# Local attention's product with v in four strips of 32 queries

## The chip, the cores and the metric

The kernel runs on one core of one Trainium2 chip. The metric is the device time of one execution in microseconds (us); lower is better. The core's engines are PE (TensorE, the matrix engine; PEld is its weight load, the load of the operand that stays in the array), DVE (VectorE), ACT (ScalarE), POOL (GpSimd) and SP (SyncE, which issues the transfers here).

## The reference

Three stages stand in a row: an attention with a sliding window, a mixture of eight dense experts, and one more two-layer network. Only the first is touched. For 4 batches and 8 heads there are 512 local and 32 global positions with a head width of 64. A local query sees the 32 global keys and the local keys at most 32 positions away:

```python
mask = np.abs(pos[:, None] - pos[None, :]) <= window
s_ll = np.where(mask, s_ll, -1000000000.0)
s_l = np.concatenate([s_lg, s_ll], axis=-1)
a_l = sm(s_l)
out_l = np.matmul(a_l, np.concatenate([v_g, v_l], axis=2))
```

The 32 global queries of each head see all 544 keys.

## The kernel before

**The attention.** The 32 (batch, head) pairs are called heads here, numbered t = 0 to 31. The 512 local queries of a head are four tiles of 128 (i = 0 to 3). For a tile, `scores` (L233, L234) makes the products with a stretch of 192 or 224 keys into the tile `s`; `maxi` (L245, DVE) adds the mask and takes the maximum; `expo` (L253, ACT) writes the exponentials `e`; `transp` (L299) transposes `e` on PE in two blocks of 112 keys into `ptp`, and a copy (L304 on ACT, L306 on DVE) brings them to `pt`. `pv` (L309) then multiplies: for each of the two blocks j, `pt` with its 112 keys by 128 queries is the weight, and the block's rows of v with a column of ones (`vw`, 112 x 65) move through the array. The two products add up in `o`, which has 128 partitions (queries) by 4 tiles by 65. `onorm` copies `o` out (L335, DVE) and divides by the column of sums.

**The global queries.** `scores_g` (L274) multiplies a head's 32 global queries with 224 and then 320 keys into `sg`; its weight has 32 columns. It is written as a generator, and `pv` lets it go one matmul further after each of its own products. `global_pv` (L363), once for every four heads, multiplies with v in 20 matmuls of 32 weight columns, each into its own 32 partitions of `og`.

**The order.** Everything in the attention stands in an order written out by hand; each engine goes through its own instructions in that order. In turn t the loop over i takes `scores`, `maxi` and `expo` of head t, `transp` of head t - 1, `pv` of tiles 0 and 1 of head t - 1 (with `scores_g` of head t between the products), and `pv` of tiles 2 and 3 of head t - 2 (with nothing between). Between such steps `fill_for` puts matmuls of the first two expert units (L131, L133, L135, and the logits at L402), which have 256 or 512 moving columns; in the first turns there are matmuls on zeros instead (L522). The attention ends at about 252 us; the experts and the last network follow and use the same engine.

**Records.** The fp32 products of `pv` and `global_pv` stand in the trace as two weight loads and two matmuls each: L316 has 512 records for 256 matmuls, L363 has 320 for 160. The names with `kh`, `sq`, `x11h` and the like are fp32r and have one record each.

Of the kernel before, what the change touches and what calls it, by code (L numbers as in the profile page):

```python
# [60 lines left out]
def tile_net(ctx: ExitStack, tc, kq, vw, vc, qg, wg, w1, w2, wi, wo, consts, out):  # L61
    nc = tc.nc
# [246 lines left out]
    def pv(t, i, between=iter(())):  # L309
        s = st[t]  # L310
        if i == 0:
            s["o"] = pso.tile([128, 4, VN], F32, tag="o", name="o")
            s["v"] = vw_t.pop(t)
        pt = s["pt", i // 2]
        for j in range(2):
            nc.tensor.matmul(  # L316
                s["o"][:, i, :], pt[:, (i % 2) * 2 + j, :], s["v"][:, i, j, :], start=(j == 0), stop=(j == 1)
            )
            next(between, None)

    def norm(o, dst):
# [185 lines left out]
    with tc.manual_schedule():  # L507
# [49 lines left out]
        for t in range(nq + 2):  # L557
# [12 lines left out]
            for i in range(4):  # L570
# [20 lines left out]
                if i >= 2:  # L591
                    between = scores_g(t, i - 2) if 0 < t < nq else iter(())
                    if 0 <= t - 1 < nq:
                        pv(t - 1, i - 2, between)
                    for _ in between:
                        pass
                if i < 2 and 0 <= t - 2 < nq:
                    pv(t - 2, i + 2)
                    if i == 1:
                        onorm(t - 2)  # L600
# [568 lines left out]
    with tc.manual_schedule():  # L1169
# [30 lines left out]
        for a, ((p, u), after) in enumerate(zip(order, order[1:])):  # L1200
# [22 lines left out]
            elif a in BACK:  # L1223
                j = BACK.index(a)
# [72 lines left out]
        for k in range(len(turns) + 1):  # L1297
# [9 lines left out]
            if k in (2, 3):  # L1307
                s = xs_[k + 1]
                side2.extend([None] * 5 + s[:5] + [None, s[5], None, s[6]])
            per = -(-len(side2) // len(seq))  # L1310
            for e in seq:
                w, i = e[0], int(e[1])
# [94 lines left out]
```

## Time and profile before

| | |
|---|---|
| time, median of 3 runs | 1983.7 us (1981.88 to 1984.66) |
| time of the profiled execution | 1985.1 us |
| span of the profiled execution | 1983.3 us |
| PE busy | 1958.3 us (99%), 11099 records |
| PE weight load busy | 1708.5 us (86%) |
| DVE, ACT, POOL busy | 1521.0, 815.1, 762.4 us |

Matmuls overlap in the array, and a record reaches from a matmul's start to the end of its results. So a record's length says less than the distance from one record's start to the next one's start, and these distances are what is read below.

### The profile page before, as it was taken

The page shows a single profiled execution, that of the slowest core. Times are in us where ns is not written, and L with a number is a line of the kernel's source. Part 1 is how long each engine was busy: PE and PEld are TensorE (multiplying, and loading weights), DVE is VectorE, ACT ScalarE, POOL GpSimd, SP SyncE. Part 2 cuts the span into 40 slices and gives each one's busy share as a digit, 9 for nine tenths or more (in the row PEclk, how much of TensorE's full clock was granted, in tenths as well). Part 3 has the DMA queues.
Part 4 walks back from the last instruction along what each step waited for, and adds up shares of the span by engine and source line. Part 5 has one row for each costly group of instructions (what it writes and reads, how often), then busy time and mean ns, then how long its engine had stood idle before and what let it go on. Part 6 is the DMA issues. An engine that isn't in the chain of part 4 may idle for free. (4 is left out here: it accounts for less than half of the span.)

```text
span 1983.3 us, 30571 instructions
## 1 busy us (share of the span) xinstructions
PE 1958.3 (99%) x11099; PEld 1708.5 (86%) x11099; DVE 1521.0 (77%) x2864; ACT 815.1 (41%) x1683; POOL 762.4 (38%) x665
## 2 busy tenths in 40 slices
PE   8999899999999999999999999999999999999999
PEld 7898887888888888899999999999999977789998
DVE  7778767776777767778888787888888668878887
ACT  6655523332333323333333334333333335545664
POOL 6665512333232333325343544445455202223322
PEclk9999999999999999999999999999999999999999
DMA  7446451123322232453333333342333396554332
GB/s 234 139 134 216 122 202 64 64 74 97 117 88 97 70 102 82 155 181 102 114 100 123 91 123 104 115 137 79 120 90 114 112 299 177 168 196 157 118 118 69
DMA packets 204518, 251.01 MB, mean 127 GB/s; under 512 B 17232, under 2 KB 150096, under 8 KB 204368
## 3 DMA queue, kind: packets, MB, share of 16 engines
q1 hardware_dynamic: 204368, 249.06, 40.0%
q8 instruction: 87, 1.43, 0.3%
q14 instruction: 63, 0.52, 0.1%
HBM read 190.16 MB, written 58.85 MB: 126 GB/s over the span
## 5 line engine op out<-in xcount | busy, mean ns | idle before, releaser
L135 PE MATMUL m<-w2h,hl 128*128 128x512 f32 x1360 | 535.2, 394 | 2.5 <-POOL hl L1056 2.5
L131 PE MATMUL m<-w2h,hh 128*128 128x512 f32 x1360 | 534.0, 393 | 2.1 <-ACT hh L1055 2.1
L133 PE MATMUL m<-w2l,hh 128*128 128x512 f32 x1360 | 533.5, 392 | 0.0
L1025 ACT ACTIVATE hh<-t 128x288 fp32r<-128x288 f32 (+1 forms) x368 | 184.8, 502 | 432.1 <-DVE t L1019 429.5
L135 PEld LDWEIGHTS m<-w2h,hl 128*128 128x128 f32 x1360 | 255.7, 188 | 58.5 <-POOL hl L1056 6.0
L131 PEld LDWEIGHTS m<-w2h,hh 128*128 128x128 f32 x1360 | 255.9, 188 | 50.6 <-ACT hh L1055 2.6
L133 PEld LDWEIGHTS m<-w2l,hh 128*128 128x128 f32 x1360 | 255.9, 188 | 49.4
L1027 DVE SCALAR_TENSOR_TENSOR hl<-t,hh 128x288 fp32r<-128x288 f32 (+1 forms) x368 | 281.0, 764 | 5.2 <-ACT hh L1025 1.5
L127 POOL TENSOR_TENSOR w2l<-w2r,w2h 128x512 fp32r<-128x512 f32 x120 | 164.2, 1393 | 300.5 <-ACT w2h L123 285.7
L1127 DVE SCALAR_TENSOR_TENSOR acc<-m,pr,acc 128x512 f32<-128x512 f32 x247 | 183.2, 746 | 113.7 <-PE m L135 112.3
L1019 DVE TENSOR_TENSOR t<-q,u 128x288 f32<-128x288 f32 (+1 forms) x348 | 182.9, 526 | 62.3 <-PE q L1086 52.6
L1056 POOL TENSOR_TENSOR hl<-eg,hh 128x288 fp32r<-128x288 f32 (+2 forms) x112 | 102.7, 924 | 290.0 <-ACT hh L1055 193.0
L743 ACT CAST wh<-wt 128x512 fp32r<-128x512 f32 x120 | 68.9, 619 | 235.1 <-POOL wt L739 235.1
L739 POOL TENSOR_TENSOR wt<-w1r,wt 128x512 f32<-128x512 f32 x60 | 89.1, 1485 | 194.4 <-DVE hl L1027 101.8
L739 POOL TENSOR_TENSOR wt<-w1r 128x512 f32<-128x512 f32 x60 | 79.8, 1334 | 164.4 <-DVE hl L1027 122.1
L1067 DVE TENSOR_TENSOR u<-q,s 128x288 f32<-128x288 f32 (+1 forms) x116 | 61.2, 527 | 83.3 <-PE q L1086 60.0
L747 DVE TENSOR_TENSOR wl<-wt,wh 128x512 fp32r<-128x512 f32 x120 | 107.1, 903 | 12.8 <-ACT wh L743 11.0
L813 POOL TENSOR_TENSOR cp<-r,cp 128x512 f32<-128x512 f32 x32 | 42.6, 1332 | 144.4 <-DVE cp L803 78.2
L1275 DVE TENSOR_TENSOR acc<-m,acc 128x512 f32<-128x512 f32 x105 | 72.1, 688 | 33.0 <-PE m L135 32.9
L253 ACT ACTIVATE e<-s,m 128x192 f32<-128x192 f32 (+1 forms) x128 | 55.7, 437 | 75.5 <-DVE m L245 74.9
L316 PEld LDWEIGHTS o<-vw,pt 112*128 112x128 f32 x512 | 77.1, 194 | 10.4 <-issue 3.8
L316 PE MATMUL o<-vw,pt 112*128 112x65 f32 x512 | 78.7, 260 | 6.2 <-issue 3.6
(248 smaller groups left out, 4665.8 us busy)
## 6 DMA issues: line engine op xcount, KB each, us to landing
w1r<-in_w_dram SPq DMA_DIRECT2D x60, 512.0 KB, 5.3
w2r<-in_w_dram SPq DMA_DIRECT2D x60, 512.0 KB, 4.2
kq<-in_kq_dram SPq DMA_DIRECT2D x31, 544.0 KB, 4.0
wh<-wqh SPq DMA_DIRECT2D x98, 128.0 KB, 2.6
wl<-wql SPq DMA_DIRECT2D x98, 128.0 KB, 2.6
r<-in_wo_dram SPq DMA_DIRECT2D x16, 512.0 KB, 4.0
r<-in_wi_dram SPq DMA_DIRECT2D x16, 512.0 KB, 4.0
vw<-in_vw_dram SPq DMA_DIRECT2D x32, 227.5 KB, 4.8
```

The source lines that it names most:

```text
L127: e.tensor_tensor(out=lo, in0=src, in1=hi.bitcast(F32), op=ALU.subtract)
L131: nc.tensor.matmul(ps, ah, bh, start=first, stop=False)
L133: nc.tensor.matmul(ps, ah, bl, start=False, stop=False)
L135: nc.tensor.matmul(ps, al, bh, start=False, stop=last)
L316: nc.tensor.matmul(s["o"][:, i, :], pt[:, (i % 2) * 2 + j, :], s["v"][:, i, j, :], start=(j == 0), stop=(j == 1))
L739: eng.tensor_tensor(out=t, in0=get(a), in1=get(b), op=op)
L747: eng.tensor_tensor(out=wop[n + "l"], in0=src, in1=wop[n + "h"].bitcast(F32), op=ALU.subtract)
L1019: nc.vector.tensor_tensor(out=t, in0=ps, in1=rest, op=ALU.add)
L1025: nc.scalar.activation(hh, t, AF.Relu)
L1027: late.append(lambda: nc.vector.scalar_tensor_tensor(out=hl, in0=t, scalar=0.0, in1=hh.bitcast(F32), op0=ALU.max, op1=ALU.subtract))
L1056: nc.gpsimd.tensor_tensor(out=hl, in0=g[:, a:b], in1=hh.bitcast(F32), op=ALU.subtract)
L1127: nc.vector.scalar_tensor_tensor(out=accs[i], in0=ps, scalar=scale, in1=accs[i], op0=ALU.mult, op1=ALU.add)
```

## The change

Each matmul of `pv` becomes four. Matmul c takes the weight columns of 32 queries and writes the 32 partitions of `o` that belong to them; the moving operand is the same 112 x 65 block of v each time.

```diff
         for j in range(2):
-            nc.tensor.matmul(
-                s["o"][:, i, :], pt[:, (i % 2) * 2 + j, :], s["v"][:, i, j, :], start=(j == 0), stop=(j == 1)
-            )
+            for c in range(0, 128, 32):
+                nc.tensor.matmul(
+                    s["o"][c:c + 32, i, :], pt[:, (i % 2) * 2 + j, c:c + 32], s["v"][:, i, j, :],
+                    start=(j == 0), stop=(j == 1),
+                )
             next(between, None)
```

There are two forms of the place on PE. In the first, with `scores_g` between the products (62 of the 128 calls of `pv`), this is what stands on PE in turn 1; the line below `pv` moves from 316 to 317, and those behind it by two:

```order
 L299 MATMUL ptp<-ident,e_139 112x128 x2
-L316 MATMUL o<-vw,pt 128x65
+L317 MATMUL o<-vw,pt 32x65 x4
 L274 MATMUL sg<-kh,sqg 32x224
-L316 MATMUL o<-vw,pt 128x65
+L317 MATMUL o<-vw,pt 32x65 x4
 L274 MATMUL sg<-kl,sqg 32x224
```

Nothing moved: four matmuls of 32 partitions stand where one of 128 stood, and the matmuls of `scores_g` stand between the two fours. In the second form, with nothing between (the other 66 calls), PE has in turn 2:

```order
 L299 MATMUL ptp<-ident,e_140 112x128 x2
-L316 MATMUL o<-vw,pt 128x65 x2
-L522 MATMUL idle<-hl 128x512
+L317 MATMUL o<-vw,pt 32x65 x8
+L524 MATMUL idle<-hl 128x512
 L299 MATMUL ptp<-ident,e_140 112x128 x2
```

Eight stand in a row where two stood. On the other engines and in the transfers the order is the one before.

## Rows read from the trace of the kernel before

**Rows 1.** Busy time in stretches: start:end, length, busy us (records), granted clock, DMA.

```profile
20.00:252.00 232.00, 221.15 (x1989) 201.21 (x1989) 176.45 (x605) 137.28 (x315) 140.16 (x158) 0.99 0.51 158
...
1000.00:1983.00 983.00, 974.80 (x5483) 866.03 (x5481) 789.50 (x1367) 421.28 (x901) 364.62 (x307) 1.00 0.43 131
```

**Rows 2.** Groups with their shapes: records, busy us, mean ns, idle before.

```profile
L316 PE MATMUL o<-vw,pt 112*128 112x65 f32 x512 | 78.7, 260 | 6.2 <-issue 3.6 <-ACT pt L304 1.9 <-ACT e L253 0.6
...
L363 PE MATMUL og<-vc,ptg 112*32 112x65 f32 x256 | 5.3, 223 | 0.0
```

**Rows 3.** PE in order of time (start us, length us, records), `global_pv` behind 512 columns.

```profile
177.26 0.40 PE L131 MATMUL m<-w2h,hh 128*128 128x512 f32 x1
177.59 0.78 PE L363 MATMUL og<-vc,ptg 112*32 112x65 f32 x40
178.30 0.50 PE L133 MATMUL m<-w2l,hh 128*128 128x512 f32 x1
178.64 0.25 PE L233 MATMUL s<-kh,sq 128*128 128x192 f32 x1
```

**Rows 4.** The same view, `global_pv` behind 256 columns.

```profile
146.64 0.28 PE L133 MATMUL m<-x22l,wh 128*128 128x256 f32 x1
146.85 0.78 PE L363 MATMUL og<-vc,ptg 112*32 112x65 f32 x40
147.56 0.39 PE L135 MATMUL m<-x22h,wl 128*128 128x256 f32 x1
147.78 0.28 PE L131 MATMUL m<-x22h,wh 128*128 128x256 f32 x1
```

**Rows 5.** The same view, `global_pv` behind `scores_g`; then one weight load there.

```profile
57.60 0.34 PE L274 MATMUL sg<-kh,sqg 128*32 128x320 f32 x1
57.78 0.33 PE L316 MATMUL o<-vw,pt 112*128 112x65 f32 x2
57.92 0.34 PE L274 MATMUL sg<-kl,sqg 128*32 128x320 f32 x1
58.19 0.79 PE L363 MATMUL og<-vc,ptg 112*32 112x65 f32 x40
...
57.63 0.34 PEld L316 LDWEIGHTS o<-vw,pt 112*128 112x128 f32 x2
```

**Rows 6.** The same view, `pv` without `scores_g`, between 512 columns.

```profile
120.27 0.48 PE L133 MATMUL m<-w2l,hh 128*128 128x512 f32 x1
120.58 0.56 PE L316 MATMUL o<-vw,pt 112*128 112x65 f32 x4
120.94 0.47 PE L135 MATMUL m<-w2h,hl 128*128 128x512 f32 x1
121.26 0.27 PE L233 MATMUL s<-kh,sq 128*128 128x224 f32 x1
```

**Rows 7.** The same view, `pv` without `scores_g`, between 256 columns.

```profile
80.66 0.28 PE L131 MATMUL m<-x11h,wh 128*128 128x256 f32 x1
80.78 0.56 PE L316 MATMUL o<-vw,pt 112*128 112x65 f32 x4
81.14 0.36 PE L133 MATMUL m<-x11l,wh 128*128 128x256 f32 x1
81.34 0.27 PE L135 MATMUL m<-x11h,wl 128*128 128x256 f32 x1
```

**Rows 8.** The same view, two expert matmuls behind each other.

```profile
116.48 0.39 PE L131 MATMUL m<-w2h,hh 128*128 128x512 f32 x1
116.71 0.40 PE L133 MATMUL m<-w2l,hh 128*128 128x512 f32 x1
```

**Rows 9.** Waits of PE's weight load, 20 to 252 us: total, times, longest.

```profile
PEld o L316 <- issue: 3.8, 1, 3.8
...
PEld og L363 <- issue: 2.0, 7, 0.4
```

**Rows 10.** The view of rows 1, one stretch (granted clock behind the counts).

```profile
204.00:211.00 7.00, 6.36 (x32) 6.39 (x32) 5.03 (x19) 3.49 (x8) 3.50 (x4) 0.52 0.50 152
```

## The prediction

> **What bounds the kernel now.** I read the busy times by stretch first. From 20 to 252 us, where the attention runs, PE is busy 221.15 of 232 us, DVE 176.45, POOL 140.16, ACT 137.28 [rows 1]: PE has 10.9 us in which nothing runs on it, every other engine 55 us or more. Behind the attention PE is busy 974.80 of 983 us [rows 1]. So PE sets the pace in the stage of the change, and what it is late at 252 us it is late at the end; the order that follows is fixed and nothing in it waits for a clock time. Then I read PE in order of time around the products in question, start to start, since the records overlap: a record of `pv` is 260 ns long on average [rows 2], but four of them and the next matmul's start take 0.36 us [rows 6, 7].
>
> The kernel already holds the form that the change introduces. `global_pv` has the same moving operand (112 x 65), the same 32 weight columns and the same four strips, 40 records at a time [rows 2, 3]. Its rows price the change.
>
> **Prices from `global_pv`.** (a) Pace. From the first start to the last end it takes 0.78 us; a record is 0.22 us long, so the last starts 0.56 us behind the first: 39 steps of 14.4 ns [rows 2, 3]. (b) Way out. The next wide matmul starts at 0.71 us, 0.15 us behind the last start, and its successor 0.34 us later [rows 3] where 0.23 us is the usual distance of 512 columns [rows 8]: 0.11 us for a weight load that was not made ahead. With 256 columns it is 0.71 again, and 0.22 us [rows 4] against 0.12 [rows 7]. (c) Way in. The first strip starts 0.33 us behind a matmul of 512 columns, 0.21 behind one of 256, 0.27 behind a `scores_g` of 320 [rows 3 to 5]; usual are 0.23, 0.12 and 0.18 [rows 8, 7, 5]. The weight load waits there for nothing that the trace names: 2.0 us in 7 places, about 0.29 us each [rows 9]. I read this as the array running empty at each change between strips and full width.
>
> **The change, call by call.** `pv` is called 128 times. It removes 256 matmuls of full width (512 records) and adds 1,024 strips (2,048 records). No wait, no transfer and no work of another engine is added.
>
> 66 calls have nothing between their products. Before: after 512 columns 0.31 us to the first record, 0.36 us to the next wide matmul, 0.32 us to its successor [rows 6]; after 256 columns 0.12, 0.36, 0.20 [rows 7]. After: 16 records take 15 x 14.4 ns = 0.22 us and 0.15 us out, 0.37 together. So the run itself gains nothing, and the ends cost: 0.33 + 0.37 + 0.34 against 0.99 is +0.05 us; 0.21 + 0.37 + 0.22 against 0.68 is +0.12 us.
>
> 62 calls have a matmul of `scores_g` behind each product. The question is whether that matmul, with 32 weight columns too, counts as a strip. The trace says no: the full-width weight of `pv` is loaded at 57.63, 0.03 us behind the start of a `scores_g` at 57.60, so these two do not stand off from each other, while `global_pv` behind a `scores_g` starts 0.27 instead of 0.18 us later [rows 5]. Then each such call goes in and out twice. A run of two records and the step to `scores_g` took 0.14 us [rows 5]; 8 strips take 7 x 14.4 ns = 0.10 and 0.15 us out: +0.11 us, twice: 0.22. The second way in costs 0.27 - 0.18 = 0.09 us. The first costs 0.33 - 0.31 = 0.02 behind 512 columns and 0.21 - 0.12 = 0.09 behind 256. The load for `scores_g` after each way out is no longer hidden; no row shows it. It has a quarter of the columns of (b), so at least 0.03 us, and at most the full 0.11; I take 0.05, nearer to the quarter, twice: 0.10. Sum: +0.43 us behind 512 columns, +0.50 behind 256.
>
> What stands ahead of a call is 512 columns, 256 columns or a transpose of 128, for which no row shows a way in; I take the middle of the two known, 0.465 and 0.085 us. 62 x 0.465 + 66 x 0.085 = 28.8 + 5.6 = **34.4 us** more on PE. All calls as behind 512 columns: 62 x 0.43 + 66 x 0.05 = 30.0; all as behind 256: 62 x 0.50 + 66 x 0.12 = 38.9. The uncertain load moves this by 124 x 0.02 = 2.5 us down or 124 x 0.06 = 7.4 us up.
>
> Something of it falls into time in which PE waits today: 10.9 us at most [rows 1], of which 3.8 us is one wait for a late `vw` transfer [rows 9] that PE would reach later, and part of the rest is waits for copies and exponentials [rows 2] whose inputs PE makes itself and would make later too. I take 5 us, with 0 and 10.9 as ends. DVE (the copy of `o` out) gets its data a fraction of a us later and has 55 us to spare.
>
> So 34.4 - 5 = +29.4 us on the profiled execution, 1985.1 to 2014.5 us. The median of the runs is 1.4 us below the profiled one: **2013 us**. Ends: 30.0 - 2.5 - 10.9 = +16.6 gives 2000; 38.9 + 7.4 = +46.3 gives 2030.
>
> **Rivals.**
> 1. `scores_g` does count as a strip once the array is in strips. Then a call with it goes in once and out once: in 0.055 on average; two runs of 8 and a step, 0.115 instead of 0.14 us, -0.05; out behind the last `scores_g` 0.09 + 0.11 = 0.20. +0.205 x 62 + 5.6 = 18.3, less 3 hidden: 1999 us. For it: the same 32 columns. Against it: rows 5. Chance 0.12.
> 2. Faster: strips run side by side and the ends cost nothing. Then 16 starts at 14.4 ns are 0.23 us for 0.36, and two runs of 8 save 0.05: 66 x 0.13 + 62 x 0.05 = 11.7 us, 1972 us. There are 66 x 2 + 62 x 4 = 380 changes of width, so it turns into a loss once one costs over 11.7 / 380 = 0.03 us. For it is the pace of 14.4 ns; against it the ends of every row of `global_pv` [rows 3 to 5]. Chance 0.04. The Trainium skill (TensorE: Matmul & The Clock Gate, section "Part 3: Packing small matmuls") reports 2.38 times the speed for three column strips of 512 moving columns; the pace in rows 3 agrees that strips overlap, and here 65 columns leave the ends to decide.
> 3. PE is less of a bound than it looks. Overlapping records hide short waits, so more than the idle 10.9 us could give way; twice that, 21.8 us, leaves +12.6, 1996 us. Against it: no other engine is over 76% busy [rows 1]. Chance 0.10.
> 4. The clock. From 204 to 211 us the granted clock is 0.52 (the level of 1.2 GHz in nearly all of it) [rows 10], right behind the 3.8 us wait [rows 9]. More places where the array runs empty may bring more such stretches; each costs at most half of its 7 us. Three more give 2023 us; the loss of this one gives 3.5 us back. Chance 0.08.
> 5. Short runs do not reach the pace of the long one. Each ns more per start costs 2,048 ns; at twice the distance, 28.8 ns, that is 29.5 us, 2042 us. Against it: 40 starts in 0.56 us, which hold ten rounds of four strips [rows 3]. Chance 0.05. The Trainium skill (the same page, section "Wait — 56ns, not 53.3ns?") says that matmuls never start less than about 25 ns apart; by that the strips would take 2,048 x 10.6 ns = 21.7 us more, 2035 us. Rows 3 differ from it, and the measurement decides here.
>
> That nothing changes at all has 0.01: the order on PE shows the four strips at every call.
>
> **How the numbers follow.** The forecast has the remaining 0.60; its own range is that of its ends, 2000 to 2030 us. The range for 8 in 10 goes from 1996 (rival 3, with rival 1 inside) to 2030 (the upper end of the sum); outside are rivals 2 and 5 and the tails. This kernel's runs scatter by about 0.1%, so 0.2% (4 us) is about what can be told from no change: slower by more than that is the forecast with rivals 1, 3, 4 and 5, nearly all of it, 0.94; within it 0.02; faster 0.04.
>
> **What would show it.** Right: the strips' records start about 14 ns apart in runs of 16 and 8; the weight load behind each run starts some 0.15 us behind the last strip and is not made ahead, also that of `scores_g` between two runs; the step from `scores_g` to a strip is about 0.3 us for 320 columns; the attention ends near 281 instead of 252 us, and from there to the end the time is what it was. Wrong: a load of `scores_g` made while strips still run (rival 1), an end of the attention at or ahead of 252 us (rival 2), the delay made good by PE waits that vanish (rival 3), new stretches at the lower clock (rival 4), or starts well over 14 ns apart (rival 5).

## The result

The changed kernel takes 2002.26 us (median of 4 runs, 2001.45 to 2002.87), the kernel before in the same comparison 1982.84 us. The ratio is 1.0097, 95% interval 1.0079 to 1.0114: 19.4 us slower. The profiled execution takes 2001.45 us.

The page's line of the changed kernel with the busy times (us, share of the span, records) shows the 1,536 added records on PE (and on its weight load, which is 22 us less busy), while the other engines are as they were but for 2 us more on DVE:

```profile
PE 1979.6 (99%) x12635; PEld 1686.1 (84%) x12635; DVE 1523.4 (76%) x2864; ACT 815.0 (41%) x1683; POOL 762.4 (38%) x665
```

What a call costs is read from PE in order of time (start us, length us, records). After the change, a call with `scores_g` between its products:

```profile
81.11 0.28 PE L133 MATMUL m<-x11l,wh 128*128 128x256 f32 x1
81.32 0.32 PE L317 MATMUL o<-vw,pt 112*32 112x65 f32 x8
81.57 0.33 PE L274 MATMUL sg<-kh,sqg 128*32 128x320 f32 x1
81.83 0.32 PE L317 MATMUL o<-vw,pt 112*32 112x65 f32 x8
82.08 0.34 PE L274 MATMUL sg<-kl,sqg 128*32 128x320 f32 x1
82.26 0.28 PE L135 MATMUL m<-x11h,wl 128*128 128x256 f32 x1
```

The same call before, first and last row:

```profile
78.39 0.28 PE L133 MATMUL m<-x11l,wh 128*128 128x256 f32 x1
...
79.15 0.28 PE L135 MATMUL m<-x11h,wl 128*128 128x256 f32 x1
```

From the expert matmul ahead to the one behind it is 1.15 us after and 0.76 us before: +0.39 us. Two ways into the strips can be seen (81.11 to 81.32, and 81.57 to 81.83, where 0.12 and 0.18 us were usual) and two ways out (0.25 us from the start of a run to the next matmul, of which the eight starts take 0.10).

The weight loads (PEld) of the same stretch show where `scores_g` stands:

```profile
81.32 0.16 PEld L317 LDWEIGHTS o<-vw,pt 112*32 112x32 f32 x8
81.57 0.11 PEld L274 LDWEIGHTS sg<-kh,sqg 128*32 128x32 f32 x1
81.83 0.16 PEld L317 LDWEIGHTS o<-vw,pt 112*32 112x32 f32 x8 [0.16 <-issue]
82.08 0.11 PEld L274 LDWEIGHTS sg<-kl,sqg 128*32 128x32 f32 x1
82.11 0.19 PEld L135 LDWEIGHTS m<-x11h,wl 128*128 128x128 f32 x1
```

The load of `scores_g` starts with its matmul at 81.57 and 82.08, not ahead of it, and so do the strips' loads; but the full-width load at 82.11 follows 0.03 us behind the `scores_g` at 82.08. So `scores_g` counts as a full-width matmul here, on both sides of the strips. Over the whole attention the strips' loads wait for nothing that the trace names (total us, times, longest; one of these waits, 3.6 us, is for a late `vw` transfer):

```profile
PEld o L317 <- issue: 23.6, 99, 3.6
```

A call with nothing between, behind 256 columns and behind 512, after the change:

```profile
83.75 0.28 PE L131 MATMUL m<-x11h,wh 128*128 128x256 f32 x1
83.96 0.44 PE L317 MATMUL o<-vw,pt 112*32 112x65 f32 x16
84.33 0.38 PE L133 MATMUL m<-x11l,wh 128*128 128x256 f32 x1
84.55 0.28 PE L135 MATMUL m<-x11h,wl 128*128 128x256 f32 x1
...
128.35 0.48 PE L133 MATMUL m<-w2l,hh 128*128 128x512 f32 x1
128.76 0.44 PE L317 MATMUL o<-vw,pt 112*32 112x65 f32 x16
129.13 0.50 PE L135 MATMUL m<-w2h,hl 128*128 128x512 f32 x1
129.47 0.27 PE L233 MATMUL s<-kh,sq 128*128 128x224 f32 x1
```

From the first to the last row of each it is 0.80 us where [rows 7] have 0.68, and 1.12 us where [rows 6] have 0.99. The run itself (its start to the next full-width start) is 0.37 us, as forecast, where it was 0.36.

In all these rows the next start comes 0.07 us ahead of the recorded end of what stands before it, wherever strips follow full width or full width follows strips: 0.28 us long and 0.21 to the next start, 0.48 and 0.41, 0.33 and 0.26, 0.32 and 0.25, 0.44 and 0.37. Where nothing changes it comes 0.16 to 0.20 us ahead (0.28 and 0.12, 0.56 and 0.36 in [rows 7]). This fits an array that has to run nearly empty at a change; the recorded ends are modelled, so it stays a reading.

Over all calls, from the last matmul ahead to the second behind, paired with the same call of before, the medians are +0.39 us for the 62 and +0.115 us for the 66: 62 x 0.39 + 66 x 0.115 = 31.8 us of price on PE.

The last product of `pv` stands at 251.7 us before and at 269.1 us after, 17.4 us later. From there to the first matmul into `q` (L1084, now L1086) it is 32.0 us in both, and from that to PE's last matmul 1695.3 and 1694.4 us: the whole loss is made in the attention, and 0.9 us of it comes back later. So in the profiled pair some 14 of the 31.8 us were absorbed. The stretches between two runs of `global_pv` show where. Before (start:end, length, busy us of PE, PEld, DVE, ACT, POOL, then the granted clock):

```profile
33.31:58.19 24.88, 22.77 (x211) 19.63 (x210) 21.07 (x74) 17.54 (x40) 19.77 (x20) 1.00 0.58 181
58.19:87.31 29.12, 27.78 (x264) 25.53 (x263) 21.35 (x80) 18.95 (x44) 18.26 (x19) 1.00 0.48 151
87.31:177.59 90.28, 89.56 (x815) 83.00 (x815) 68.69 (x245) 52.72 (x124) 55.95 (x66) 1.00 0.49 146
177.59:249.04 71.45, 65.18 (x544) 58.67 (x543) 52.78 (x167) 38.30 (x87) 35.30 (x44) 0.95 0.53 166
```

After:

```profile
34.64:59.63 24.99, 24.70 (x402) 17.31 (x401) 19.94 (x72) 17.37 (x40) 18.70 (x19) 1.00 0.59 174
59.63:91.42 31.79, 31.21 (x457) 23.36 (x456) 21.07 (x78) 19.15 (x44) 17.89 (x19) 1.00 0.42 131
91.42:192.58 101.16, 100.75 (x1392) 76.50 (x1391) 72.00 (x245) 52.74 (x123) 56.00 (x66) 1.00 0.45 132
192.58:266.29 73.71, 69.73 (x928) 52.47 (x927) 52.36 (x167) 38.21 (x87) 35.54 (x44) 0.98 0.52 159
```

Four heads (8 calls of each kind) carry a price of 8 x 0.39 + 8 x 0.115 = 4.0 us; the four stretches hold 4, 4, 12 and 8 heads. The third, where PE was idle 0.7 of 90 us, grows by 10.9 of 12 us: almost the whole price. The second grows by 2.7 of 4.0 us. The first grows by 0.1 of 4.0 us, and its idle time falls from 2.1 to 0.3 us. The last grows by 2.3 of 8 us: its idle time falls from 6.3 to 4.0 us, and the clock gives back about 2 us: (1 - 0.95) x 71.45 = 3.6 us of clock were missing before [rows 10], (1 - 0.98) x 73.71 = 1.5 us after. Ahead of 33 us the delay is 1.3 us for a price of 3.8; there the kernel before had another stretch at the lower of the two clock levels, from 9.5 to 16.5 us at 0.51, which began in a wait of 2.2 us for `sqg`; the changed kernel, which waited 1.6 us there, had 1.00.

PE's waits in the attention show which of them went (total us, times, longest; `issue` where the trace names no instruction). Before:

```profile
PE o L316 <- issue: 3.6, 1, 3.6
PE ptp L299 <- DVE pt L306: 2.4, 6, 0.7
PE o L316 <- ACT pt L304: 1.9, 4, 0.8
```

After:

```profile
PE o L317 <- issue: 3.8, 2, 3.4
PE o L317 <- ACT pt L304: 0.8, 2, 0.5
PE ptp L299 <- DVE pt L306: 0.3, 2, 0.2
```

The wait for the late `vw` transfer stayed (the longest `issue`, 3.6 and 3.4 us): this transfer was issued 16.3 us later too. What shrank are the waits for the copies `pt` and the exponentials, from 6.0 to 1.1 us with the rows not shown. Such a wait costs more than its idle time: at 55.98 us before, a `scores_g` started 0.85 us behind the product ahead of it, of which 0.52 us show as idle, and after the change 0.25 us. Added up start to start, the 128 calls are 25.0 us longer and not 31.8, the steps into the transposes (L299) are 5.4 us shorter and all other steps 2.2 us shorter: 17.4 us.

The other three executions of the changed kernel had a mean clock of 0.997 to 0.998 instead of 0.999, and their times lie within 1.4 us of the profiled one. By the medians 12 of the 31.8 us were absorbed, and the clock can have given some 2 us of this (an estimate: 0.001 of 2000 us, since the executions of the kernel before have 0.996 to 0.998).

### The profile page after: what moved, and what is told of

Read it like the earlier page. It is cut to its first block, busy times and chain, and to the rows that moved or that the text cites. A ratio compares the mean times of both kernels' runs of the same rounds, so it can differ in the third digit from the quotient of the medians.

```text
span 1999.7 us, 33643 instructions
## 1 busy us (share of the span) xinstructions
PE 1979.6 (99%) x12635; PEld 1686.1 (84%) x12635; DVE 1523.4 (76%) x2864; ACT 815.0 (41%) x1683; POOL 762.4 (38%) x665
## 5 line engine op out<-in xcount | busy, mean ns | idle before, releaser
L1067 ACT COPY s<-q 128x288 f32<-128x288 f32 (+1 forms) x116 | 51.9, 447 | 74.9 <-PE q L1088 74.9
L1039 ACT ACTIVATE er<-t 128x288 f32<-128x288 f32 (+1 forms) x96 | 48.5, 505 | 81.9 <-DVE t L1021 81.8
```

## Experiments

Theory A: each change between strips and full width costs time, because the array runs empty there, and `scores_g` counts as full width, so a call pays two changes or four; PE's waits absorb a part. Theory B: what costs is the number of matmul records. Each run below was timed beside the kernel before; ratios are with 95% intervals. In the code cuts, `...` stands for lines left out.

**Strips in one kind of call only.** In the first run, only for tiles 2 and 3, where nothing stands between the products; in the second (with `i < 2` in the line below), only for tiles 0 and 1.

```diff
-            for c in range(0, 128, 32):
+            n = 32 if i >= 2 else 128
+            for c in range(0, 128, n):
                 nc.tensor.matmul(
-                    s["o"][c:c + 32, i, :], pt[:, (i % 2) * 2 + j, c:c + 32], s["v"][:, i, j, :],
+                    s["o"][c:c + n, i, :], pt[:, (i % 2) * 2 + j, c:c + n], s["v"][:, i, j, :],
...
```

> Strips only in the 64 calls for tiles 2 and 3 (nothing between the products); the other 64 at full width. Theory A (the array runs empty at every change of width): the changed kernel's trace prices such a call at 0.115 us of PE, so 64 x 0.115 = 7.4 us on PE, of which about half falls into waits: +3 to +7 us over the kernel before. Theory B (the number of records costs, wherever they stand): half of the added records, so half of the +19.4 us: about +10 us.

> Strips only in the 64 calls for tiles 0 and 1, 62 of which have scores_g behind each product. Theory A: 62 x 0.386 us = 24 us on PE, of which about half falls into waits: +12 to +17 us. Theory B (the number of records): half of the +19.4 us, about +10 us.

Measured: 1986.40 us against 1982.44, ratio 1.0022 (1.0014 to 1.0031), +4.0 us; and 1997.22 us, ratio 1.0072 (1.0059 to 1.0085), +14.8 us. Both add the same number of records, and one costs nearly four times the other. B falls. The two add up to 18.8 us, and the change measured 19.4.

**Fewer changes with the same records.** The two matmuls of `scores_g` stand behind both products; once with strips, once at full width as the control.

```diff
-                        pv(t - 1, i - 2, between)
+                        pv(t - 1, i - 2)
```

> All calls in strips, the two matmuls of scores_g behind both products instead of one behind each, so that an sg call goes into strips and out once, not twice. To be compared with the same order at full width. Theory A: two changes of width fewer in 62 calls, 0.27 us each: 128 calls at 0.115 us = 15 us on PE over the control, about half of it absorbed: +6 to +11 us. Theory B (the number of records): the same +19 us over its control as the change has.

> The kernel before with the two matmuls of scores_g behind both products: the control for the run with strips in that order. Both theories: within 3 us of the kernel before, since the same matmuls stand on PE and none changes width.

Measured: 1991.90 us with strips, 1983.89 us at full width (ratio to the kernel before 1.0003, 0.9994 to 1.0012). The strips cost 8.0 us in this order and 19.4 in the other. So two changes less in each of 62 calls are worth 11 us, with as many records.

**Half as many records, as many changes.** Two matmuls of 64 weight columns for each product.

```diff
-            for c in range(0, 128, 32):
+            for c in range(0, 128, 64):
                 nc.tensor.matmul(
-                    s["o"][c:c + 32, i, :], pt[:, (i % 2) * 2 + j, c:c + 32], s["v"][:, i, j, :],
+                    s["o"][c:c + 64, i, :], pt[:, (i % 2) * 2 + j, c:c + 64], s["v"][:, i, j, :],
...
```

> Two matmuls of 64 weight columns instead of four of 32, in every call: as many changes of width as the change, half of its added records (512 instead of 1,536 more matmul records). Theory A (the change of width costs): about what the change costs, +15 to +21 us over the kernel before. Theory B (the number of records costs): a third of it, about +6 us.

Measured: 2004.53 us against 1984.19, ratio 1.0103 (1.0089 to 1.0117), +20.3 us, as much as with four strips, though the added records are a third (512 for 1,536). PE in order of time of this run:

```profile
84.98 0.28 PE L131 MATMUL m<-x11h,wh 128*128 128x256 f32 x1
85.19 0.45 PE L317 MATMUL o<-vw,pt 112*64 112x65 f32 x8
85.57 0.38 PE L133 MATMUL m<-x11l,wh 128*128 128x256 f32 x1
85.80 0.28 PE L135 MATMUL m<-x11h,wl 128*128 128x256 f32 x1
```

The way in (0.21 us), the run with its way out (0.38) and the load behind it (0.23) are those of the strips of 32.

**Added time without strips.** At full width, the first product of each call for tiles 0 and 1 is made three times, and the first two results are overwritten.

```diff
         for j in range(2):
-            nc.tensor.matmul(
-                s["o"][:, i, :], pt[:, (i % 2) * 2 + j, :], s["v"][:, i, j, :], start=(j == 0), stop=(j == 1)
-            )
+            for k in range(3 if i < 2 and j == 0 else 1)[::-1]:
+                nc.tensor.matmul(
+                    s["o"][:, i, :], pt[:, (i % 2) * 2 + j, :], s["v"][:, i, j, :], start=(j == 0), stop=(j == 1 or k > 0)
+                )
```

> The kernel before, where the first product of each call for tiles 0 and 1 is made three times (the first two are thrown away; the outputs stay the same): 64 calls with four more full-width records, 0.11 us each, so 64 x 0.44 = 28 us more on PE without any change of width. The change has about 32 us more on PE by its own trace and is 19 us slower. If PE's waits for other work absorb added time of any kind (theory A), 28 us come out as +13 to +19 us; if the absorbed part came from strips alone (rival: strips shorten something else), they come out as +25 to +28 us.

Measured: 2003.26 us against 1984.19, ratio 1.0099 (1.0085 to 1.0113), +19.1 us for 28 us of added PE time. So absorbing is not peculiar to strips, and added time at full width is absorbed as well: 9 of 28 us here, 12 of 32 in the change (by the medians), 3 of 7 and 9 of 24 in the two partial changes. The share that comes out is 0.54 to 0.68 in all of them.

**Longer runs.** First all four tiles of a head in one run of 32 strips, then two tiles in one run of 16, each with its control at full width. In both, no `scores_g` stands between the products.

```diff
-                    if 0 <= t - 1 < nq:
-                        pv(t - 1, i - 2, between)
...
                 if i < 2 and 0 <= t - 2 < nq:
-                    pv(t - 2, i + 2)
+                    for k in range(4) if i == 0 else ():
+                        pv(t - 2, k)
```

> All four tiles of a head in one run of 32 strips (64 records), without scores_g between: 2 changes of width per head instead of 12. To be compared with the same order at full width. Theory A: a run of 64 starts takes 63 x 14.4 ns = 0.91 us, with 0.15 out and some 0.2 us for way in and the load behind it 1.26 us; 16 records at full width take about 1.7 us. So 0.4 us less per head, 32 heads: 6 to 14 us faster than its control, the lower end if PE then waits more. Theory B (the number of records costs): about 19 us slower than its control.

> The kernel before with the four tiles of a head in one run of products at full width: the control for the grouped strips. Both theories: within 6 us of the kernel before; the same matmuls in another order.

Measured: 1975.94 us with strips, ratio to the kernel before 0.9961 (0.9947 to 0.9974); 1995.80 us at full width, 1.0057 (1.0045 to 1.0070). Strips win 19.9 us in this order, more than A's 6 to 14. PE in order of time with strips:

```profile
93.80 0.48 PE L135 MATMUL m<-w2h,hl 128*128 128x512 f32 x1
94.21 1.13 PE L317 MATMUL o<-vw,pt 112*32 112x65 f32 x64
95.27 0.50 PE L131 MATMUL m<-w2h,hh 128*128 128x512 f32 x1
95.61 0.39 PE L133 MATMUL m<-w2l,hh 128*128 128x512 f32 x1
```

and in the control:

```profile
93.98 0.48 PE L133 MATMUL m<-w2l,hh 128*128 128x512 f32 x1
94.29 1.90 PE L316 MATMUL o<-vw,pt 112*128 112x65 f32 x16
96.00 0.47 PE L135 MATMUL m<-w2h,hl 128*128 128x512 f32 x1
96.31 0.39 PE L131 MATMUL m<-w2h,hh 128*128 128x512 f32 x1
```

From the first to the last row it is 1.81 against 2.33 us: 0.52 us less per head, 17 us for 32 heads. The ends cost what they cost before (0.41 in, 0.34 behind), but now 64 records share them. The other 3 us go with the clock, as far as the recorded executions tell: the profiled control had a granted clock of 0.96 from 20 to 252 us, the run with strips 0.98, and the two executions with a mean clock of 0.998 (1992.24 and 1975.65 us) lie 16.6 us apart, the two with 0.997 (1993.39 and 1975.94) 17.5.

That the control is 11.6 us slower than the kernel before was not expected. Its PE waits more for DVE's copy of the transposed exponentials (total us, times, longest), 7.3 and 2.1 us against 2.4 and 0.7 in the kernel before; the run with strips has nearly the same (6.6 and 2.3), so these waits come with the order. The rest of the 11.6 us was not traced.

```profile
PE ptp L299 <- DVE pt L306: 7.3, 11, 1.3
PE s L233 <- DVE pt L306: 2.1, 3, 1.3
```

With two tiles in a run:

```diff
-                    if 0 <= t - 1 < nq:
-                        pv(t - 1, i - 2, between)
+                    if 0 <= t - 1 < nq and i == 3:
+                        pv(t - 1, 0)
+                        pv(t - 1, 1)
...
                 if i < 2 and 0 <= t - 2 < nq:
-                    pv(t - 2, i + 2)
                     if i == 1:
+                        pv(t - 2, 2)
+                        pv(t - 2, 3)
```

> Two tiles of a head in one run of 16 strips (32 records), scores_g behind it: 4 changes of width per head. To be compared with the same order at full width. Theory A: by the traces so far a run costs a step in that is 0.09 us longer than at full width and a step behind it 0.02 to 0.1 us longer, and 32 starts with the way out take 31 x 14.4 ns + 0.15 = 0.60 us against 0.82 us for 8 records at full width. So some 0.11 us less per run, 64 runs: 7 us less on PE than the control, 3 to 8 us faster than it. Runs of 16 strip records lost (+8 us against their control) and runs of 64 won (-20), so A says that the sign turns between 16 and 32 records. Theory B (the number of records costs): some 8 us slower than its control, as with runs of 16.

> The control: two tiles of a head in one run of products at full width, scores_g behind it. Both theories: within 6 us of the kernel before; grouping all four tiles at full width cost 11 to 12 us, in which PE waited more for the copies of the transposed scores; this order moves tiles 0 and 2 by one step only.

Measured: 1977.90 us with strips, ratio 0.9972 (0.9963 to 0.9981); 1981.59 us at full width, 0.9997 (0.9988 to 1.0006). Strips win 3.7 us. So against the same order at full width, runs of 16 records lose 8.0 us, runs of 32 win 3.7 and runs of 64 win 19.9 (some 17 at the same clock). The two kernels with longer runs of strips beat both the kernel before and the change; the best, with one run per head, is 8.2 us (0.39%) faster than the kernel before.

## Why the prediction was right, and where it was off

It said 2013 us, 1996 to 2030, slower; measured were 2002.3 us, and +19.4 us where +29.4 was forecast. The mechanism was the one forecast, by its own steps; that the sum on PE came out so near is partly luck:

- **The pace and the run.** 16 strips with the way out take 0.37 us, as worked out from `global_pv`; the strips save nothing in a run of 16. In runs of 16 and of 8 the last start follows the first by 0.22 and 0.10 us (record 0.22 us long), 14 to 15 ns a step. Rival 5 (short runs miss the pace) falls. So does rival 2: the ends decide.
- **`scores_g` counts as full width.** The loads at 81.57 and 82.11 show it, and the run with `scores_g` behind prices it. Rival 1 falls.
- **The price on PE** was 34.4 us and is 31.8. Two terms were off, in opposite directions. The load of `scores_g` behind a run, put at 0.05 us twice, costs nothing: the way from `scores_g` into the second strips is 0.26 us with it, where [rows 5] have 0.27 without it, so 62 x 0.10 = 6.2 us were too much. And a call between 512 columns costs 0.13 us in the rows above (0.12 in the median of such calls), not 0.05: the expert matmul ahead of it in [rows 6] starts its record about 0.08 us early behind a transpose (it is 0.48 us long, not 0.40 as in [rows 3]), so the way in from [rows 3] may not be put beside that distance. The same 0.08 us is missing in the calls with `scores_g` behind 512 columns, for which 0.02 us was put as the first way in and 0.10 was measured (0.41 for 0.31).
- **The step that was mis-sized** is "I take 5 us, with 0 and 10.9 as ends": some 12 us of the price were absorbed by the medians, which lies outside these ends and is more than all the idle time of [rows 1]. The prediction had its parts the wrong way round: the 3.8 us wait for `vw`, which it took as one that PE would reach later, stayed, and the waits for copies and exponentials, which it expected to stay since PE makes their inputs, nearly went. A likely reason is that PE's added work stands between making an input and needing what becomes of it, so the engine that copies it has that time too; no run separates this. The trace shows idle time falling by about 5 us in the four stretches, and full-width matmuls that add 28 us come out as 19. Rival 3 had this mechanism (records hide short waits) and gave it 21.8 us; the truth lies between. It is not spread evenly: from 87 to 178 us nearly all of the price comes out, ahead of 58 and behind 178 us little of it. So the attention ended at 269 and not near 281 us.
- **Rival 4** (more stretches at the lower clock) is not seen: in the attention the changed kernel had one, about 222 to 226 us (0.57), behind its 3.4 us wait, where the profiled execution before had two of 7 us (0.51 and 0.52).

Left open is why `scores_g` with its 32 columns does not count as a strip (it is fp32r, and alone), so the width alone is not what makes a change; no run varied it.

## What to carry to other kernels

Splitting a matmul's weight into strips of columns pays only for a run long enough to carry its ends: here a run of 16 short records breaks even in itself and loses its ends, one of 32 wins a little, one of 64 wins clearly. So first bring such products together, and count changes between strips and full width, not matmuls. When time is added to the busiest engine of a stage with several coupled engines, the visible idle time need not be the limit of what is absorbed; a matched dose of dummy work on the same engine measures it.

## What the hardware showed that was not expected

- Strips start some 14.5 ns apart on average over 64, 40, 16 and 8 records alike, and a run of halves of 64 columns takes nearly the same time as one of strips of 32 (0.38 for 0.37 us), with the same ends.
- A weight load of 32 columns behind the way out does not lengthen it: the 0.11 us read for 128 columns in [rows 3] are not seen for `scores_g` (0.26 us from its start to the next strip, against 0.27 in [rows 5]).
- A matmul with 32 weight columns in fp32r next to full-width ones pays for no change (a full-width load follows 0.03 us behind its start), while next to fp32 strips of 32 columns it does, in both directions (0.26 us in, 0.25 us for a run of eight with its way out).
